# RWKV-7 recurrence and SwiGLU feed-forward on one core: copies of chunks 0 to 3 and a step of the weights' narrowing on GpSimd, token loads of chunks 1 to 3 on SyncE, another written-out order

## Chip, cores and metric

The kernel runs on one core of one Trainium2 chip. The metric is device time in microseconds of one execution of the whole program, as the median of several runs. Engines are named as the profile names them: PE (TensorE, PEld its weight loads), DVE (VectorE), ACT (ScalarE), POOL (GpSimd) and SP (SyncE, which here only issues DMAs).

## The reference

Two parts follow each other. The first is a recurrence over 768 tokens for 4 x 8 heads of 40 dimensions, with a 40 x 40 state per head:

```
for t in range(S):
    y[:, :, t] = einsum('bhd,bhde->bhe', r_t, state)
    Sa = einsum('bhde,bhe->bhd', state, a_t)
    state = state * w_t[:, :, None, :] - einsum('bhd,bhe->bhde', Sa, b_t) \
            + einsum('bhd,bhe->bhde', v_t, k_t)
```

The second takes y as 3072 rows of 320: x / sqrt(mean(x*x) + 1e-6) * rms_g, then silu(xn @ w_gate) * (xn @ w_val) @ w_out with 1536 hidden columns. The three weight matrices come as 64-bit floats, the other inputs as 32-bit.

## The kernel before, in words

The recurrence is cut into 24 chunks of C = 32 tokens, and for each chunk the work is written in stages:

- `front(c)` loads the chunk's tokens (tiles `wan`, with w and a; `kbn`, with k and b; `VU`, with v), turns them on PE, and builds what does not depend on the state. It runs through five levels, l = 1, 2, 4, 8, 16. At each level ACT copies keys from `K` into `KE`, PE makes a `gram` of `KE` and `A`, DVE writes its lower part into `LT` (a predicated copy, `where`), ACT copies another part into `KN`, DVE multiplies `K` in place, and the next level's `A` is made (at l = 16 it is `aP`). Half of the next `A` is the old one's values, moved to other places: the kept half, a copy of 128 x 256 elements on ACT (`copy(a1...)`, lines 513 and 523). The other half is a product on DVE. After the last level two copies of 128 x 512, `e0` and `e1` (lines 541 and 542), bring the last-level keys into `KE`; PE turns `KE`, and ACT copies the result into `KN` 32. There is one tile `KE`, so the next chunk's first key copy must wait for that turn.
- `inverse(c)` and, for chunks 0 to 3, `early_inverse(c)` invert the chunk's triangular matrices: `LT` goes out to the DRAM tile `sB` and comes back as `M`, DVE runs a chain of small products and subtractions (`tmp`, `M` or `Yi`), and the result goes out through `sY` and back.
- `main(c)` needs the state after chunk c - 1, the inverse and `front(c)`; it updates the state, makes `y`, the squared sum (`ss`), `x`, and the scaled and turned `xg`.
- `narrow(f, h)` makes 32-bit weights of half of weight tile `w` f, 24 halves in all: loads issued by POOL into a tile that is not yet in use, three steps of the exponents on ACT (into `ex`, or `o` where that tile is lent; lines 772 to 774), and three steps on DVE.
- `feed(g)` is the feed-forward part for two chunks, 12 in all: 12 weight tiles each, matmuls `ps<-xg,w`, silu on ACT (`sg`), product on DVE (`hT`), and `po<-w,hT`. The first, `feed(0)`, needs `main(0)` and `main(1)`.

None of it is issued as it is written. Every piece of work goes into a `Plan` with its engine, and `ORDER`, a table of numbers written out by hand or by a program, says in which order the pieces are issued; `PAIRS` says in which of three pairs of PSUM banks a temporary stands. Each engine works through its own pieces in that order and waits on semaphores for the others. A word "-" in `ORDER` issues a warming matmul on PE (`po<-ident`, line 1010), which computes nothing that is used.

Helpers, by whose lines the profile groups work: `copy` (476), `scale` (479), `act` (473) on ACT; `tt`, `where`, `ts`, `stt` (all 453) on DVE; `ptt` (482), `pcopy` (485), `blank` (488) on POOL; `dma` (492); `mm` (495) and `flip` (498) on PE. Buffer numbers are left out in the profile; in order rows `K_128` is the first of two `K` tiles.

Which queue loads a chunk's tokens is decided in two lines: chunk 0 by SP and ACT, chunk 1 by SP except its `VU`, and all later chunks by POOL.

Of the kernel before, what the change touches and what calls it, by code (L numbers as in the profile page):

```python
# [18 lines left out]
C = 32  # L19
# [4 lines left out]
EARLY, LATE = 4, 6  # L24
# [9 lines left out]
363 362 58 54 55 60 59 56 6 5 391 44 46 28 133 4 39 7 8 40 72 53 10 196 364 367 9 368 68 57 365 193 27 11 13 366 185  # L34
188 184 74 73 69 75 373 12 14 15 369 388 380 70 189 16 17 18 66 183 71 81 80 372 79 84 389 83 42 - - 82 187 93 91 88 76
90 182 78 89 92 20 41 195 34 262 35 85 94 186 321 65 77 102 98 99 103 64 100 87 399 201 43 203 86 101 104 108 109 263
202 477 473 398 95 97 110 476 472 114 105 198 470 475 107 113 112 96 115 197 390 474 118 106 116 199 129 126 117 119
130 111 212 125 222 232 200 120 124 123 - 242 121 211 131 204 134 210 132 208 209 205 - 220 206 213 214 219 207 489 381
471 218 217 223 63 127 128 221 215 824 823 228 227 51 229 233 224 231 67 225 230 819 820 226 491 490 240 237 241 29 320
238 194 30 371 234 216 236 243 239 135 62 61 136 137 138 139 140 141 142 248 143 486 - - 244 235 144 145 247 146 147  # L40
488 382 259 246 148 149 258 249 150 245 151 152 153 154 155 156 36 21 370 254 253 487 260 255 0 156 157 158 159 160 161
251 162 163 835 491 1006 821 1002 338 1007 18 391 392 492 836 496 165 166 37 164 167 249 498 495 837 500 260 497 499
493 121 494 506 310 - 504 505 508 168 501 256 394 509 510 519 507 515 502 311 255 384 321 511 382 373 263 514 518 376
817 512 517 516 520 503 377 264 265 525 521 513 176 172 174 170 177 816 323 374 44 178 169 173 171 175 179 523 375 250
47 31 30 266 267 268 269 524 270 21 530 46 957 526 191 820 528 529 385 522 180 378 383 399 531 534 545 393 312 - 36 313
324 407 32 405 315 537 271 272 532 956 386 395 314 316 325 535 416 533 - 317 408 415 322 326 329 549 49 318 546 330 331
336 400 402 527 273 274 275 276 396 277 278 279 538 280 281 282 283 284 540 541 285 286 287 288 289 290 333 335 403 547
401 339 417 404 332 337 334 342 344 838 2 539 1 291 423 406 548 409 340 190 189 341 420 292 345 421 542 543 544 484 550
551 832 294 426 412 552 553 834 293 410 554 346 347 413 481 425 424 434 411 414 427 536 844 418 295 - 343 348 349 833
# [5 lines left out]
468 580 879 958 615 614 621 887 886 582 0 263 92 - - 261 93 267 259 517 525 602 266 603 604 0 647 538 290 94 316 267 95  # L55
# [10 lines left out]
765 770 79 0 221 572 14 0 381 382 16 761 570 359 - 77 576 - 383 281 17 579 0 370 566 752 106 750 0 0 427 63 0 203 204  # L66
205 213 366 564 367 562 565 559 570 563 558 63 59 207 746 102 104 211 427 60 368 569 288 429 1 3 0 62 759 564 367 368 0
367 759 569 571 368 570 369 580 370 576 208 202 205 758 564 371 259 57 563 260 0 371 567 2 0 371 - 59 208 60 204 202
259 0 207 0 0 569 368 206 207 61 996 274 277 62 369 575 370 371 372 373 374 375 376 420 422 421 424 584 561 423 275 256
0 0 375 376 377 378 379 380 381 382 577 569 570 578 55 0 55 254 0 0 - 380 381 382 383 568 577 384 420 422 423 421 0 0  # L70
559 574 561 529 266 578 0 575 559 584 423 582 55 382 428 426 51 425 583 383 - 578 568 384 385 386 581 387 429 388 389
52 595 570 390 594 424 56 0 524 390 426 568 0 578 577 390 1 0 983 0 2 - 425 427 416 987 986 0 581 0 414 0 384 385 587
# [306 lines left out]
def kernel(  # L379
# [33 lines left out]
    nc = tc.nc  # L413
# [70 lines left out]
    def pcopy(o, a):  # L484
        plan.add("POOL", "copy", lambda at: nc.gpsimd.tensor_copy(o, a), [o], [a])
# [557 lines left out]
```

## Time and profile before

| | |
|---|---|
| median of 3 runs | 932.68 us (931.99 to 933.84) |
| the profiled execution | 934.37 us, of which 932.6 from the first to the last instruction |
| mean granted TensorE clock in it | 0.991 |
| busy in it: PE, PEld | 875.7 us (94%), 703.2 us (75%) |
| DVE, ACT, POOL | 723.2 us (78%), 521.9 us (56%), 294.9 us (32%) |
| DMA, mean over the span | 68 GB/s |

A profile shows one execution. Groups of instructions are given as: line, engine, operation, output tile <- input tiles, shapes, count, then busy time, mean duration of one in ns, and the engine's idle time just before, with what ended it. Rows of waits read: who waited, for whom, total us, times, longest. Rows of the timeline and the chain of waits begin with the start in us and the duration. Rows of stretches give each engine's busy time and, in brackets, its number of instructions. A busy PE is not PE at its peak, since ends of matmuls are modelled, and spans on POOL are rough.

### The profile page before, as it was taken

Reading aid. Unit: us, or ns where it says so; the run is one execution under the profiler, and the core shown is the slowest. Engines: PE = TensorE matmul, PEld = TensorE weight load, DVE = VectorE, ACT = ScalarE, POOL = GpSimd, SP = SyncE. Lnnn points to the kernel's source line nnn. Section 1 sums busy time; section 2 is a strip of 40 time slices with the busy share of each in tenths; the row PEclk is TensorE's granted clock in tenths of the full one; section 3 lists DMA queues with packets and bytes.
Section 4 is the critical chain, followed back from the end, with each engine's and each line's share of the span. In section 5 each row is a group of like instructions: output and inputs, shape, how many; then the busy total and the mean of one; then the engine's idle time right before and its main releaser. Section 6 shows DMA issues by size and latency. Waiting matters only on the chain.

```text
span 932.6 us, 50195 instructions
## 1 busy us (share of the span) xinstructions
PE 875.7 (94%) x22072; PEld 703.2 (75%) x22072; DVE 723.2 (78%) x2702; ACT 521.9 (56%) x1144; POOL 294.9 (32%) x515
## 2 busy tenths in 40 slices
PE   4776898899999999999999999999999999999998
PEld 4665776677777788777777887887787777878776
DVE  5887778878878888978888888888888887864511
ACT  5887877674555566565555655655545454432211
POOL 8576546404221323432221333412503320200000
PEclk9999999899999999999999999999999999999999
DMA  9653546223242243333323223413414222021000
GB/s 162 104 119 84 126 98 153 73 69 67 55 87 49 46 86 73 71 59 60 70 39 74 64 54 75 89 35 71 88 21 85 61 41 62 11 60 28 3 15 15
DMA packets 146363, 63.01 MB, mean 68 GB/s; under 512 B 128800, under 2 KB 138080, under 8 KB 146144
## 3 DMA queue, kind: packets, MB, share of 16 engines
q1 hardware_dynamic: 125664, 29.46, 17.1%
q0 software_dynamic: 18368, 30.01, 15.1%
q8 instruction: 173, 2.83, 1.3%
q10 hardware_dynamic: 2112, 0.33, 0.3%
q14 instruction: 46, 0.38, 0.1%
HBM read 49.15 MB, written 10.09 MB: 64 GB/s over the span
## 4 chain that ended last, share of the span: by engine, by line
PE 72%; DMA 9%; DVE 6%; ACT 6%; issue 3%; SPq 2%; POOL 1%; DVEq 0%; POOLq 0%; ACTq 0%
PE ps L495 50%; PE po L495 14%; PE ps L498 7%; SPq L492 2%; DMA M<-sB 2%; DMA w<-in_moe_w_out_dram 1%; DMA LT<-sY 1%; DMA w<-in_moe_w_gate_dram 1%; DVE tmp L453 1%; DVE y L453 1%; DMA sY<-Yi 1%; ACT VU L476 1%; ACT KE L476 1%; DVE Yi L453 1%; DMA sY<-M 1%
## 5 line engine op out<-in xcount | busy, mean ns | idle before, releaser
L495 PE MATMUL ps<-xg,w 128*128 128x256 f32 (+1 forms) x1728 | 354.2, 393 | 1.2 <-DVE Yi L453 0.5
L495 PEld LDWEIGHTS ps<-xg,w 128*128 128x128 f32 (+1 forms) x1728 | 263.7, 191 | 49.1 <-issue 12.4
L495 PE MATMUL po<-w,hT 128*128 128x320 f32 x576 | 179.0, 449 | 0.0
L492 POOL DMA_DIRECT2D VU<-in_v_dram x184 | 102.4, 560 | 172.7 <-PE ps L495 78.1
L453 DVE TENSOR_TENSOR tmp<-Yi,M 128x60 f32<-128x60 f32 (+24 forms) x620 | 129.3, 209 | 20.5 <-DMA M<-sB 6.1
L453 DVE TENSOR_TENSOR Yi<-Yi,tmp 128x60 f32<-128x60 f32 (+24 forms) x620 | 129.7, 210 | 13.8
L473 ACT ACTIVATE sg<-ps 128x256 f32<-128x256 f32 x144 | 52.6, 384 | 150.6 <-PE ps L495 143.1
L495 PEld LDWEIGHTS po<-w,hT 128*128 128x128 f32 x576 | 106.0, 192 | 37.4 <-issue 1.9
L476 ACT COPY KE<-K 128x512 f32<-128x512 f32 x168 | 110.6, 662 | 26.2 <-DVE K L453 18.2
L453 DVE TENSOR_TENSOR hT<-ps,sg 128x256 f32<-128x256 f32 x144 | 58.3, 420 | 68.7 <-ACT sg L473 57.4
L453 DVE TENSOR_TENSOR K<-K,T 128x256 f32<-128x256 f32 x240 | 98.9, 421 | 10.2 <-ACT KE L476 8.8
L495 PE MATMUL ps<-A,KE 40*64 40x72 f32 x3840 | 95.0, 247 | 9.0 <-ACT KE L476 1.7
L495 PEld LDWEIGHTS ps<-A,KE 40*64 40x64 f32 x3840 | 79.2, 149 | 28.9 <-issue 9.3
L476 ACT COPY KN<-ps 128x320 f32<-128x320 f32 x144 | 67.4, 471 | 59.1 <-PE ps L495 28.5
L453 DVE COPY_PREDICATED LT<-msk,ps 128x256 f32<-128x256 uint32 x120 | 65.9, 550 | 19.5 <-PE ps L495 10.2
L482 POOL TENSOR_TENSOR ss<-ss,mhalf 128x1 f32<-128x1 f32 x24 | 15.4, 641 | 194.2 <-DVE ss L453 179.2
L453 DVE TENSOR_TENSOR y<-y,ps 128x256 f32<-128x256 f32 x119 | 49.9, 419 | 11.0 <-PE ps L495 7.9
L453 DVE TENSOR_TENSOR A<-A,T 128x128 f32<-128x128 f32 (+1 forms) x168 | 55.8, 335 | 1.5 <-ACT A L476 0.4
L495 PEld LDWEIGHTS ps<-As,KN 64*40 64x40 f32 x3840 | 45.1, 123 | 12.7 <-issue 4.4
L495 PE MATMUL ps<-As,KN 64*40 64x32 f32 x3840 | 50.3, 204 | 3.1 <-DVE y L453 1.6
L476 ACT COPY VU<-ps 32x320 f32<-32x320 f32 x96 | 40.0, 417 | 15.5 <-PE ps L495 14.2
L492 POOL DMA_DIRECT2D wan<-in_w_dram x44 | 29.1, 661 | 57.4 <-PE ps L498 57.1
(121 smaller groups left out, 1250.2 us busy)
## 6 DMA issues: line engine op xcount, KB each, us to landing
M<-sB SPq DMA_DIRECT2D x80, 128.0 KB, 3.4
rn<-in_r_dram SPq DMA_DIRECT2D x24, 160.0 KB, 4.6
out_dram<-o SPq DMA_DIRECT2D x48, 80.0 KB, 2.3
VU<-in_v_dram POOLq DMA_DIRECT2D x184, 20.0 KB, 2.6
kbn<-in_b_dram POOLq DMA_DIRECT2D x44, 80.0 KB, 3.4
kbn<-in_k_dram POOLq DMA_DIRECT2D x44, 80.0 KB, 3.3
wan<-in_w_dram POOLq DMA_DIRECT2D x44, 80.0 KB, 3.1
wan<-in_a_dram POOLq DMA_DIRECT2D x44, 80.0 KB, 3.3
```

The lines of the kernel that those rows point to most:

```text
L453: plan.add("DVE", kind, lambda at: fn(at(o), *m(at)), [o], aps(*args))
L473: plan.add("ACT", "act", lambda at: nc.scalar.activation(at(o), at(a), f, **kw), [o] + aps(acc), [a])
L476: plan.add("ACT", "copy", lambda at: nc.scalar.copy(at(o), at(a)), [o], [a])
L482: plan.add("POOL", "tt", lambda at: nc.gpsimd.tensor_tensor(o, a, b, op), [o], [a, b])
L492: plan.add(by, "dma", lambda at: queue.dma_start(out=o, in_=i), [o], [i])
L495: return o, lhsT, rhs, lambda at: nc.tensor.matmul(at(o), lhsT, rhs, start=start, stop=stop, skip_group_check=True)
L498: return o, i, ident, lambda at: nc.tensor.transpose(at(o), i, ident)
```

## The change

A new constant, `SOON = 4`. For chunks 0 to 3, `front` makes the kept halves of `A` (and `aP`) and the two last-level key copies `e0` and `e1` with `pcopy`, on POOL, where it used `copy`, on ACT: 5 + 2 copies for each chunk, 28 in all. For chunks 1 to 3 all token loads are issued by SP: 8 more `VU` loads of chunk 1, and 8 token loads and 8 `VU` loads of each of chunks 2 and 3, 40 in all, leave POOL's queue. The last of the three exponent steps of `narrow`, a multiplication of integers by 2 to the 23rd, goes from ACT to POOL for all 24 halves. And `ORDER` and `PAIRS` are other tables.

```
-EARLY, LATE = 4, 6
+EARLY, LATE, SOON = 4, 6, 4
...
-0 225 226 223 0 0 0
+222 226 223 224 225 0 - 0 0
...
+    def pts(o, a, by, op):
+        plan.add("POOL", "ts", lambda at: nc.gpsimd.tensor_scalar(o, a, by, None, op), [o], [a])
...
     def tokens(t, i, x, src, tk, by="SP"):
-        dma(..., by if tk.start == 0 else "SP" if tk.start == C else "POOL")
+        dma(..., by if tk.start == 0 else "SP" if tk.start < SOON * C else "POOL")
...
     def front(c):
+        move = pcopy if c < SOON else copy
...
-                        "SP" if c == 0 else "POOL")
+                        "SP" if c < SOON else "POOL")
...
-                copy(a1[:, :, :, 0], a0[:, :, 0])
+                move(a1[:, :, :, 0], a0[:, :, 0])
...
-                copy(a1[:, :, :, :, 0], a0[:, :, 0].rearrange("p n f s l -> p n s f l"))
+                move(a1[:, :, :, :, 0], a0[:, :, 0].rearrange("p n f s l -> p n s f l"))
...
-        copy(e0, K[:, 0].rearrange("p (m n) (x t) -> p m n x t", m=2, x=2))
-        copy(e1, ap(K, N * 2 * C + C, (4 * 2 * C, 2), (2 * C, 4), (-C, 2), (1, C)))
+        move(e0, K[:, 0].rearrange("p (m n) (x t) -> p m n x t", m=2, x=2))
+        move(e1, ap(K, N * 2 * C + C, (4 * 2 * C, 2), (2 * C, 4), (-C, 2), (1, C)))
...
-        act(ex, ex, AF.Copy, scale=2.0 ** 23)
+        pts(ex, ex, 2.0 ** 23, MUL)
```

The tables move pieces on every engine. Three places show how. PE's pieces are the same in number and kind, 28 warming matmuls among them.

ACT, before, from the end of chunk 0's front (keys `K_128`, `KN_0`) into chunk 1's (`K_129`):

```order
L476 COPY KE<-K_128 128x2x4x2x32
L476 COPY KN_0_117<-ps_65 128x320
L476 COPY KE<-K_128 128x2x4x2x32
L476 COPY A_132<-ps_64 128x8x64
L476 COPY aP_133<-A_131 128x16x16
L476 COPY KE<-K_129 128x512
L476 COPY A_131<-A_132 128x8x32
```

ACT, in the changed kernel, from the same level of chunk 0 to the same first key copy of chunk 1:

```order
L477 COPY KN_0_117<-ps_65 128x320
L477 COPY KN_0_114<-ps_64 128x320
L474 ACTIVATE o_170<-w_164,ctop 128x480
L474 ACTIVATE ex_172<-w_163,ctop 128x480
L474 ACTIVATE o_170<-o_170,cmid 128x480
L477 COPY KE<-K_129 128x512
```

The two key copies, the `aP` copy and chunk 1's first `A` copy are no longer on ACT, and exponent steps of two weight tiles stand ahead of chunk 1's first key copy.

POOL, before, while chunk 0's front is made: loads of tokens of chunk 2 and of weights:

```order
L492 DMA kbn_96<-in_b_dram 32x16x40 x2
L492 DMA w_162<-in_moe_w_gate_dram 128x2x256
L492 DMA kbn_96<-in_k_dram 32x16x40 x2
L492 DMA wan_95<-in_w_dram 32x16x40
L492 DMA wan_95<-in_a_dram 32x16x40
L492 DMA VU_99<-in_v_dram 32x4x40
L492 DMA w_165<-in_moe_w_gate_dram 64x256
```

POOL, in the changed kernel, from the end of chunk 0's front into chunk 1's:

```order
L489 COPY KE<-K_128 128x2x4x2x32 x2
L489 COPY aP_133<-A_131 128x16x16
L496 DMA w_165<-in_moe_w_gate_dram 64x256
L496 DMA w_162<-in_moe_w_out_dram 128x448
L489 COPY mid<-msk 128x256
L489 COPY M_135<-ident 32x8x16
L496 DMA w_162<-in_moe_w_gate_dram 128x2x256
L489 COPY A_131<-A_132 128x8x32
L489 COPY A_132<-A_131 128x8x16x2
```

The token loads are gone from POOL; the copies stand there among loads of weights and the filling of constants.

SP, before, where chunk 0's `LT` goes out to `sB_173` and comes back as `M_135`:

```order
L492 DMA sB_173<-LT_102 32x8x32 x4
L492 DMA VU_98<-in_v_dram 32x4x40
L492 DMA M_135<-sB_173 32x16x16 x2
L492 DMA VU_98<-in_v_dram 32x4x40
L492 DMA rn_97<-in_r_dram 64x16x40
```

SP, in the changed kernel, there:

```order
L496 DMA sB_173<-LT_102 32x8x32 x4
L496 DMA kbn_96<-in_k_dram 32x16x40
L496 DMA VU_98<-in_v_dram 32x4x40
L496 DMA wan_95<-in_a_dram 32x16x40
L496 DMA wan_95<-in_w_dram 32x16x40
L496 DMA M_135<-sB_173 32x16x16
L496 DMA kbn_96<-in_k_dram 32x16x40
L496 DMA M_135<-sB_173 32x16x16
```

Token loads of chunks 2 and 3, which wait until PE has turned the chunk before and so freed their tile, now stand between the two transfers.

More of the change, by code (lines that the diff above doesn't have):

```diff
@@ new lines @@
+235 144 145 146 487 488 245 147 148 247 149 386 150 392 393 246 151 152 194 66 - 836 311 312 259 249 258 260 193 321
[5 rows of a table added]
+405 533 280 281 282 283 284 285 286 326 524 534 318 327 330 331 332 337 - 287 425 408 426 427 428 535 288 289 290 291
+292 293 431 319 818 2 190 822 328 429 340 335 333 334 338 191 821 48 1007 453 546 547 336 540 295 341 432 342 294 329
+548 343 344 296 409 410 411 1008 430 433 346 347 348 542 297 195 541 192 349 413 52 435 412 350 833 839 834 414 415 345
+549 835 452 847 843 23 857 481 543 - 1020 840 1021 454 842 351 352 353 957 1001 1006 844 848 841 867 354 538 599 434
@@ new lines @@
+298 444 463 484 482 537 846 544 442 460 355 845 302 443 854 356 1022 436 853 545 480 552 855 553 554 455 555 456 556
+600 849 856 852 864 49 858 866 306 862 601 863 457 877 437 851 865 557 - 859 1005 445 462 558 559 560 561 876 304 850
[4 rows of a table added]
+272 271 270 274 275 276 293 277 278 659 0 309 660 317 316 2 1 272 278 659 293 904 535 671 279 280 533 532 540 0 157 - -
[6 rows of a table added]
+76 12 366 - 265 364 184 77 254 579 369 267 377 565 313 372 371 370 376 269 268 263 78 271 270 0 14 15 579 12 265 580
+263 372 373 374 378 575 272 274 0 12 15 16 305 17 773 0 377 579 224 273 271 269 0 78 273 274 275 278 276 277 16 770 1
@@ new lines @@
+17 574 378 279 767 769 126 224 306 307 768 2 379 380 79 225 226 381 363 280 19 382 281 282 383 384 20 283 80 227 18 0
+307 227 581 570 0 263 427 - 558 63 562 561 99 564 0 363 364 558 564 565 559 206 210 211 102 574 569 571 59 60 566 - -
+568 570 575 427 567 573 365 366 367 743 744 1 429 368 369 263 63 264 66 370 265 64 584 572 371 580 372 3 0 0 0 0 260
+206 201 203 207 65 573 0 569 0 259 260 570 577 206 0 0 0 0 571 - 49 55 565 577 361 578 362 363 364 365 366 367 570 368
+369 583 203 60 569 257 204 205 260 258 53 749 0 0 749 368 369 370 748 257 577 416 371 372 373 374 580 375 376 377 991 1
@@ new lines @@
+741 783 784 988 785 989 0 434 617 828 832 439 830 829 785 786 787 788 831 835 995 789 440 836 833 834 790 - 991 791 792
+793 992 1008 993 839 1093 794 840 795 796 841 797 - 435 798 842 799 845 847 846 1138 1394 682 943 939 844 800 441 801
[7 rows of a table added]
+1195 0 545 592 593 655 594 651 746 654 595 652 747 596 4 657 656 658 653 597 598 660 743 659 760 599 744 600 - 0 600
[28 rows of a table added]
+1159 817 818 819 820 430 - 1217 1166 1 683 1083 1084 1086 1170 1171 1167 1174 1026 1027 1028 1029 1176 1172 863 864 434
+1030 1181 824 822 1031 1185 1032 1033 1195 1034 1180 441 1169 - 436 1186 823 437 1035 865 866 867 1168 1036 821 1087
@@ L242 @@
-42220044024200200400200442020422400000444420204
+20404240010220204445204204204422440242244040404244202242200042024014540040400402404000202000444220020022004420404204044
+42000044422042242400000224200402242242242224420444444204404240424020244240024040240002240000422444400402442204040242240
+44440444040240220240444444002400422402422202040024222442024200042024420400420024024242040440044222200002002424224422042
+20442200020042442420440204424444200020424224424402422440204240202240422400440400404244424202022404022000002200244400022
@@ L243 @@
+22000402002022002244004204444224424444240240042
 """
@@ L657, in tokens @@
     def tokens(t, i, x, src, tk, by="SP"):
-        dma(flat(t)[rows(i, x), :, 0:D], src[2 * i:2 * i + 2, :, tk, :].rearrange("q h s d -> s (q h) d"), by if tk.start == 0 else "SP" if tk.start == C else "POOL")
+        dma(flat(t)[rows(i, x), :, 0:D], src[2 * i:2 * i + 2, :, tk, :].rearrange("q h s d -> s (q h) d"), by if tk.start == 0 else "SP" if tk.start < SOON * C else "POOL")
     def front(c):
```

53 lines of the change are left out of this document (14 added, 39 removed), and 332 rows, old and new, of the table ORDER.

## The prediction

> **What bounds the kernel now.** I read the table of stretches first, cut at the first matmul (9.6 us), at the first matmul of the feed-forward part (112.4 us) and at 193 us, when the last weights are narrowed.
>
> ```profile
> 0.00:9.60 9.60, 0.00 (x0) 0.00 (x1) 2.68 (x7) 3.09 (x4) 8.30 (x27) 1.00 0.83 139
> 9.60:112.40 102.80, 77.14 (x2213) 66.96 (x2213) 83.60 (x277) 83.25 (x174) 64.80 (x119) 1.00 0.62 118
> 112.40:193.00 80.60, 73.18 (x1943) 57.59 (x1940) 65.34 (x218) 59.42 (x122) 41.25 (x69) 0.94 0.47 105
> 193.00:932.60 739.60, 725.41 (x17920) 578.69 (x17920) 571.60 (x2204) 376.16 (x847) 180.50 (x302) 1.00 0.28 55
> 112.39 3.79 PE L495 MATMUL ps<-xg,w 64*128 64x256 f32 x16
> ```
>
> After the length, the columns are busy time of PE, PEld, DVE, ACT and POOL, then the granted clock. PE does nothing for 9.6 us, idles 102.8 - 77.1 = 25.7 us in the second stretch, which I call the ramp, and then 7.4 and 14.2 us. PE's work is not touched by the change (as many matmuls, as many warming ones), so the end moves only by what PE's idle time gains or loses, and nearly half of that (25.7 of 56.9) is in the ramp. There DVE (83.6) and ACT (83.3 of 102.8) are both about 81% busy, and POOL 63%.
>
> Next the table of waits, for the ramp alone: first PE's, then DVE's.
>
> ```profile
> PE ps L498 <- DVE y L453: 4.1, 2, 2.5
> PE ps L495 <- ACT M L476: 3.6, 3, 2.7
> PE ps L498 <- ACT KE L476: 2.4, 2, 1.6
> PE ps L498 <- ACT VU L476: 2.4, 2, 1.7
> PE ps L495 <- ACT KE L476: 1.7, 2, 1.2
> PE ps L495 <- ACT A L476: 1.5, 2, 1.0
> PE ps L495 <- ACT KN L476: 1.5, 2, 1.0
> PE ps L498 <- ACT vut L476: 1.2, 1, 1.2
> PE ps L498 <- ACT r L476: 1.0, 1, 1.0
> ...
> DVE K L453 <- ACT KE L476: 4.4, 4, 3.2
> DVE w L453 <- ACT ex L473: 3.4, 1, 3.4
> DVE As L453 <- ACT As L479: 1.9, 1, 1.9
> DVE ss L453 <- ACT x L473: 1.1, 1, 1.1
> ```
>
> The eight ACT rows of PE add up to 15.3 of its 25.7 us; the DVE row is 4.1. DVE itself idles 102.8 - 83.6 = 19.2 us, and its four ACT rows are 10.8 of them. So in the ramp ACT is most often what is late. The chain of waits shows why, where chunk 0's front ends and chunk 1's begins:
>
> ```profile
> 24.28 0.62 ACT KE L476
> ...
> 25.22 0.52 ACT KE L476
> 25.74 0.49 ACT A L476
> 26.23 0.31 ACT aP L476
> 26.54 0.86 ACT KE L476
> ```
>
> From 24.28 on ACT does one copy after another, and PE's next gram waits for the last (26.54 and 0.86 long). Those of 0.62, 0.52 and 0.31 us, at 24.28, 25.22 and 26.23, are among the ones that the change moves.
>
> **The change, part by part.** ACT loses, for chunks 0 to 3, 20 kept-half copies (tiles A and aP), 8 key copies (KE), and one of three exponent steps of every half weight tile, 24 in all.
>
> ```profile
> L476 ACT COPY KE<-K 128x512 f32<-128x512 f32 x28 | 18.5, 660 | 6.1 <-PE ps L495 3.1 <-DVE K L453 2.9
> L476 ACT COPY A<-A 128x256 f32<-128x256 f32 x16 | 6.8, 422 | 0.3 <-DVE A L453 0.3
> L473 ACT ACTIVATE ex<-ex 128x480 int32<-128x480 int32 x8 | 4.8, 604 | 0.1
> ```
>
> All 28 copies and 12 of the exponent steps stand ahead of the first feed: 20 x 0.422 + 8 x 0.660 + 12 x 0.604 = 21 us. ACT's instructions overlap at their ends (the chain counts 0.31 for an aP copy), so I take 17 us off its busy time: 83.3 becomes 66, and its free time in the ramp 19.5 becomes 36.5. If waits behind ACT fell only as its load, PE would get back 15.3 x 17 / 83.3 = 3.1 us; if they went altogether, 15.3. A queue's waits go rather as busy time over free time, 4.3 before and 1.8 after, which leaves 0.43 of them: I take 15.3 x 0.57 = 8.8 us, and 3.1 and 15.3 as ends.
>
> The rows of ACT's order in the section on the change show the place of that chain: the two key copies, the aP copy and the first A copy of chunk 1 are gone from ACT, and steps for weights fill their place. The key copies are not off the path, though: both must be done before PE can turn KE, and only then may K_129's copy write KE again. On ACT the pair took 25.74 - 24.28 = 1.5 us, with a KN copy in the part left out.
>
> POOL takes them. What it does with such shapes, and what its DMA issues cost, the groups of POOL in the ramp show:
>
> ```profile
> L492 POOL DMA_DIRECT2D VU<-in_v_dram x14 | 8.0, 569 | 0.4 <-PE ps L495 0.4
> L567 POOL TENSOR_SCALAR_AFFINE_SELECT eye<-eye 32x256 f32<-32x256 f32 x4 | 2.0, 509 | 0.3
> L485 POOL COPY mid<-msk 128x256 f32<-128x256 f32 x3 | 1.3, 431 | 1.6 <-DVE msk L453 1.6
> ```
>
> A kept half is a copy of 256 elements: 0.43 us, as on ACT. A key copy has 512: between 0.51, the select's time for 256, and twice 0.43 (0.86); I take 0.65, since some of 0.43 is fixed, so the pair is 1.3 us against 1.5. No row has an integer multiply on POOL; 480 elements lie between 0.51 again and the select scaled up (0.509 x 480 / 256 = 0.95); I take 0.70, near what 0.65 for 512 and a slower operation make. Before the first feed the change has 28 copies and 14 exponent steps on POOL: 20 x 0.43 + 8 x 0.65 + 14 x 0.70 = 23.6 us (19.8 to 28.8 by the ends). 32 loads leave POOL there, by the VU row at 0.57 us or more: 18 us. POOL so goes from 64.8 to about 70 of 102.8 and does not become the bound; but its new work stands in line with loads that wait. In the rows of POOL's order, token loads, which waited for PE to free their tiles, are replaced by copies; but the load into w_162, which waits until DVE has narrowed what lay there, stands ahead of chunk 1's A copies. I charge 1 us for copies held up so, with 0 and 5 as ends.
>
> The larger cost is on DVE. Rows of the timeline, POOL's copies beside DVE's work:
>
> ```profile
> 13.14 0.40 POOL L485 COPY mid<-msk 128x256 f32<-128x256 f32 x1 [1.59 <-DVE msk L453]
> 13.49 0.65 POOL L485 COPY A<-ident 40x320 f32<-40x320 f32 x1
> 13.31 1.10 DVE L453 TENSOR_TENSOR K<-K,T 128x256 f32<-128x256 f32 x2 [0.30 <-ACT T L476]
> 19.06 0.76 DVE L453 TENSOR_TENSOR K<-K,T 128x256 f32<-128x256 f32 x2 [0.16 <-ACT KE L476]
> 33.19 0.54 POOL L488 MEMSET y<- 128x512 f32 x1
> 33.18 0.49 DVE L453 TENSOR_TENSOR A<-A,T 128x128 f32<-128x128 f32 x2
> ```
>
> Under two POOL copies (1.05 us) the pair of K products took 1.10 us instead of 0.76: 0.34 lost, 0.32 us for each us of copying. Under a memset, which reads nothing, the A products ran on at 0.49 for two. At 0.32 the new reading on POOL costs DVE 23.6 x 0.32 = 7.6 us in the ramp; the ends are 0 (copies that fall into DVE's idle time) and 14.4 (below). What PE sees of it is less, since PE waits less for DVE than for ACT: I take half, 3.8 us.
>
> The 40 loads on SP:
>
> ```profile
> 11.18 0.98 SPq L492 DMA_DIRECT2D kbn<-in_k_dram  x2
> ...
> sB<-LT SPq DMA_DIRECT2D x16, 32.0 KB, 3.4
> ```
>
> 0.49 us each, 20 us on a queue that mostly waits. In the rows of SP's order four loads now stand between sB_173 and the first M_135; 4 x 0.49 = 2.0 us is covered by the 3.4 us that the sB transfer needs to land. I charge nothing; without that cover, as when a load there waits for PE to free its tile, it is 2 us, twice, for the two inverses ahead of the first feed: 4 us.
>
> After 112.4 us ten or twelve exponent steps leave ACT too, with 7.4 us of PE's idle time to be had in that stretch; I charge nothing there, with -2 to +2 as ends, since DVE (65.3 of 80.6) is the busier.
>
> **The sum**, made against the profiled execution: its span of 932.6 us and 1.8 around it make 934.37, 0.2% over the median of the runs, 932.68. The terms are -8.8 (ACT) + 3.8 (DVE) + 1 (POOL's line) + 0 (SP) = -4.0 us; 930.4 against the profiled execution, 928.7 against the median, which I forecast.
>
> **The rivals.** First, slower: **POOL's reads hold up DVE.** If every copy blocks DVE for as long as it runs whenever DVE wants two operands, DVE loses 23.6 us times its busy share (0.81) times the share of such work. That share is bounded by the groups of DVE in the ramp that do not read two tiles of SBUF (LT's reads its mask and PSUM):
>
> ```profile
> L453 DVE COPY_PREDICATED LT<-msk,ps 128x256 f32<-128x256 uint32 x20 | 10.9, 547 | 5.2 <-PE ps L495 4.6 <-ACT KN L476 0.4
> L453 DVE TENSOR_SCALAR w<-w 128x480 int32<-128x480 int32 x13 | 5.8, 449 | 3.4 <-ACT ex L473 3.4
> L453 DVE TENSOR_TENSOR y<-y,ps 128x256 f32<-128x256 f32 x9 | 3.8, 419 | 2.2 <-PE ps L495 2.1
> ```
>
> These are 20.5 of 83.6, so the share is at most 0.755 and the loss 23.6 x 0.81 x 0.755 = 14.4 us. DVE gets back 10.8 x 0.57 = 6.2 of its waits for ACT; if DVE sets the ramp, the end comes 8.2 us later: 940.9. It decides from 6.2 / 23.6 = 0.26 us of DVE for each us of POOL upward, if DVE and not ACT is then what is late; the measured 0.32 is just over that, DVE's share of PE's waits speaks against. The Trainium skill, "SBUF — State Buffer", section "Who interferes with whom", says that a DVE instruction with two SBUF inputs and a GpSimd instruction that reads SBUF exclude each other entirely, while one that only writes does not matter. By that rule this rival is what happens; the trace agrees on both halves (1.10 instead of 0.76 us beside copies, 0.49 for two beside a memset). Chance 0.25.
>
> Second, **no difference**: the same balance at 0.32 gives DVE +7.6 - 6.2 = +1.4 us, and with DVE 81% busy before, a freer ACT only moves the wait: 932.7 to 934.1. Chance 0.17, counting as no difference what is within 0.2% (1.9 us), about what a measurement of this kernel can tell.
>
> Third, **faster by more**: PE gets nearly all its ACT waits back (-15.3), POOL's copies fall into DVE's free time, and 3 us are charged for all else: -12, 920.7. For it speaks that the line of copies on ACT at each change of chunk is cut short; against it, that PE can turn KE only after the same key copies. Chance 0.13.
>
> Fourth, **lines on POOL and SP**: A copies behind loads that wait for DVE (5), M behind token loads (4), against half the ACT gain (-4.4): +4.6, 937.3. Chance 0.08.
>
> **How the numbers follow.** The forecast, 924 to 931, has 0.37. Faster by over 0.2%: 0.37 + 0.13 = 0.50; within: 0.17; slower: 0.25 + 0.08 = 0.33. Both signs hold much of this, so the range takes in the third rival's value and the first's: 920 to 941, with about 0.15 outside.
>
> **What would show it.** Right: in the changed profile the first xg matmul starts about 4 us before 112.4, PE's waits ended by ACT in the ramp fall from 15.3 to about 6.5, KE copies of 512 elements take about 0.65 us on POOL and exponent steps about 0.7, K products beside them are lengthened by about a third of POOL's time. Wrong: the first feed at 112 us or later with DVE over 92 us busy before it and PE's waits now ended by DVE or POOL (first rival); rows of A or aP on POOL that start long after their input is there, with a load ahead (fourth); exponent steps well over 1 us, which would make POOL the bound; or a gain of the ramp that comes back as PE idle time between 112 and 193 us.

## The result: 27 us slower, and where the profile shows it

The changed kernel takes 959.76 us (median of 4 runs, 957.10 to 965.79) against 932.34: a ratio of 1.0301, 95% interval 1.0263 to 1.0340. I had forecast 928.7, and 920 to 941 as the range. The profiled execution took 960.75 us, of which 958.8 are its span.

The table of stretches of the changed kernel, cut at the first matmul of the feed-forward part (121.8) and at the end of `feed(0)`'s last output matmul (230.2); columns as in the prediction (length, busy PE, PEld, DVE, ACT, POOL, granted clock):

```profile
9.60:121.80 112.20, 75.81 (x2191) 65.35 (x2187) 95.44 (x278) 69.40 (x137) 84.36 (x131) 1.00 0.60 110
121.80:230.20 108.40, 93.77 (x2398) 73.41 (x2396) 79.74 (x258) 63.87 (x137) 55.19 (x72) 0.87 0.38 87
230.20:958.80 728.60, 714.27 (x17473) 569.35 (x17472) 559.29 (x2153) 366.05 (x818) 177.95 (x298) 1.00 0.27 54
```

The same view of the kernel before, from its first feed to the same matmul:

```profile
112.40:206.10 93.70, 85.66 (x2299) 67.40 (x2296) 76.11 (x254) 69.63 (x148) 43.57 (x73) 0.95 0.45 102
```

The first feed comes 9.4 us later, not 4 earlier: PE idles 112.2 - 75.8 = 36.4 us there instead of 25.7, less 1.3 us of work that it now does ahead of 9.6. Between the cuts it idles 14.6 instead of 8.0 us, +6.6. Over the whole span its idle time goes from 56.9 to 73.6 us, +16.7, and its busy time, for the same matmuls, from 875.7 to 885.2, +9.5. 16.7 + 9.5 are the 26.2 us of the two spans. The second part I put down to the clock, 0.87 between the cuts instead of 0.95: 0.13 x 108.4 less 0.05 x 93.7 is 9.4 us that half clock took more, an estimate from these rows, which takes it that all of PE's work there is paced by the clock.

POOL's groups up to 125 us have the new work:

```profile
L486 POOL TENSOR_SCALAR ex<-ex 128x480 int32<-128x480 int32 x9 | 13.3, 1479 | 3.5 <-ACT ex L474 3.4
...
L489 POOL COPY A<-A 128x256 f32<-128x256 f32 x16 | 9.2, 574 | 8.5 <-DVE A L454 5.6 <-DVE T L454 0.9 <-PE ps L499 0.8
...
L486 POOL TENSOR_SCALAR o<-o 128x480 int32<-128x480 int32 x5 | 7.2, 1442 | 5.1 <-ACT o L474 5.0
L489 POOL COPY KE<-K 128x512 f32<-128x512 f32 x8 | 5.6, 707 | 5.6 <-PE ps L499 3.3 <-DVE K L454 1.5 <-DVE tmp L454 0.8
```

The exponent step takes 1.44 to 1.48 us, twice the 0.70 that I took and well over my upper end of 0.95; on ACT it was 0.60. The 14 of them are 20.5 us of POOL.

And the waits from 9.6 to 121.8 us, the first rows of PE's and of ACT's:

```profile
PE ps L499 <- ACT KE L477: 6.3, 4, 2.6
PE ps L499 <- ACT M L477: 4.1, 4, 2.0
PE ps L499 <- ACT rE L477: 4.0, 1, 4.0
...
ACT KE L477 <- DVE K L454: 12.4, 10, 2.1
ACT K L477 <- PE ps L502: 8.0, 3, 6.2
```

PE's waits ended by ACT did not shrink, though ACT's load fell as forecast: three rows alone are 14.4 us, against 15.3 for the eight rows of ACT before, and PE now waits for copies on POOL too (4.2 us). ACT itself waits for DVE's K products ahead of its key copies (12.4 us; 2.9 before), so the row names the last engine of a chain, not the slow one.

### The profile page after: what moved, and what is told of

Same layout as the page of the kernel before. It is cut to its first block, busy times and chain, and to the rows that moved or that the text cites. A ratio compares the mean times of both kernels' runs of the same rounds, so it can differ in the third digit from the quotient of the medians.

```text
span 958.8 us, 50223 instructions
## 1 busy us (share of the span) xinstructions
PE 885.2 (92%) x22072; PEld 709.3 (74%) x22072; DVE 739.6 (77%) x2702; ACT 501.6 (52%) x1092; POOL 326.3 (34%) x527
## 4 chain that ended last, share of the span: by engine, by line
PE 68%; DVE 10%; ACT 8%; DMA 7%; issue 3%; POOL 2%; SPq 1%; ACTq 0%; DVEq 0%; POOLq 0%
PE ps L499 47%; PE po L499 14%; PE ps L502 7%; DMA kbn<-in_k_dram 2%; ACT VU L477 2%; DVE tmp L454 2%; SPq L496 1%; DVE w L454 1%; DVE K L454 1%; ACT KE L477 1%; DVE LT L454 1%; DVE hT L454 1%; DVE Yi L454 1%; ACT KN L477 1%; DMA sY<-M 1%
## 5 line engine op out<-in xcount | busy, mean ns | idle before, releaser
L496 POOL DMA_DIRECT2D VU<-in_v_dram x160 | 88.7, 558 | 143.7 <-PE ps L499 88.1
L477 ACT COPY KE<-K 128x512 f32<-128x512 f32 x160 | 105.8, 662 | 50.5 <-DVE K L454 40.9
L454 DVE TENSOR_TENSOR K<-K,T 128x256 f32<-128x256 f32 x240 | 99.5, 424 | 15.3 <-ACT KE L477 9.6
L477 ACT COPY KN<-ps 128x320 f32<-128x320 f32 x144 | 67.2, 469 | 73.6 <-DVE LT L454 29.0
L499 PE MATMUL ps<-As,KN 64*40 64x32 f32 x3840 | 53.2, 206 | 9.5 <-DVE y L454 3.8
L454 DVE TENSOR_TENSOR y<-y,T 128x256 f32<-128x256 f32 x96 | 41.5, 433 | 2.8 <-ACT y L477 1.2
```

Of the source, the lines that this page charges most:

```text
L454: plan.add("DVE", kind, lambda at: fn(at(o), *m(at)), [o], aps(*args))
L477: plan.add("ACT", "copy", lambda at: nc.scalar.copy(at(o), at(a)), [o], [a])
L496: plan.add(by, "dma", lambda at: queue.dma_start(out=o, in_=i), [o], [i])
L499: return o, lhsT, rhs, lambda at: nc.tensor.matmul(at(o), lhsT, rhs, start=start, stop=stop, skip_group_check=True)
```

## The experiments

Times are given as a ratio to the kernel before on the same chip, with its 95% interval, and as that share of 932.7 us.

### Which part costs what

Four kernels: the new tables (`ORDER`, `PAIRS`) with parts of the moves undone, and the old tables with one part. Exponents back on ACT, in the changed kernel:

```
-        pts(ex, ex, 2.0 ** 23, MUL)
+        act(ex, ex, AF.Copy, scale=2.0 ** 23)
```

> The changed kernel with one line undone: the exponents' last step is on ACT again; copies on GpSimd, loads on SyncE and the new order stay. Theory E (the exponent step, 1.4 to 1.5 us on POOL where I had 0.70, is the cause: it fills POOL and holds DVE): at least half of the 27 us comes back, 933 to 946 us, first feed at 112 to 116 us, DVE lengthened by 7 us instead of 15. Theory P (each read of POOL blocks DVE, the copies as much as the exponents): about half of it, 944 to 952. Theory O (the new order and the loads on SP lose it): within 4 us of the changed kernel, 956 to 964, since ACT only gets its 14 us of work back.

Measured: 953.86 us, 1.0209 (1.0186 to 1.0232), 19.5 us. It lies between what P and what O gave (952 and 956), and none of the three is met: about 9 of the 28 us are the exponents'.

Copies back on ACT, in the changed kernel:

```
-        move = pcopy if c < SOON else copy
+        move = copy
```

> The changed kernel with the kept halves and the key copies of chunks 0 to 3 on ACT again; the exponent step stays on GpSimd. Theory E: little comes back, 952 to 960, since POOL only goes from 81 to about 67 us busy before the first feed. Theory P: 940 to 950, DVE lengthened by 10 us instead of 15. Theory O: 956 to 966.

Measured: 964.82 us, 1.0322 (1.0294 to 1.0351), 30 us; not told apart from the changed kernel, in O's range.

New tables alone: both edits above, and

```
-        dma(..., by if tk.start == 0 else "SP" if tk.start < SOON * C else "POOL")
+        dma(..., by if tk.start == 0 else "SP" if tk.start == C else "POOL")
...
-                        "SP" if c < SOON else "POOL")
+                        "SP" if c == 0 else "POOL")
```

> The new order alone: exponents and copies on ACT, token loads of chunks 2 and 3 on GpSimd as before. Theory O: it keeps at least half of the loss, 946 to 965. Theories E and P: the order costs little by itself, 930 to 940; above 934 because the order was made for other engines.

Measured: 961.66 us, 1.0295 (1.0272 to 1.0318), 27.5 us, in O's range. The tables lose by themselves all that the change loses.

The kernel before, with only the exponents' step on POOL:

```
-        act(ex, ex, AF.Copy, scale=2.0 ** 23)
+        pts(ex, ex, 2.0 ** 23, MUL)
```

> The kernel before, in its own order, with only the exponents' last step on GpSimd. Theory E: slower by half of the 27 us or more, 946 to 965, with POOL at 64.8 + 14 x (1.4 to 1.6) = 84 to 87 us busy before the first feed. Theory P: 940 to 948 (35 us of reading at 0.22 to 0.32 us of DVE each, half of it in the ramp). Theory O: 928 to 936, no loss without the new order.

Measured: 966.41 us, 1.0347 (1.0312 to 1.0381), 32 us, just above E's range. So the exponents too lose by themselves all that the change loses, in the old order. The two do not add. The other parts in the old order, each with the lines of the change's diff for it; first all moves, without the new tables:

```
+        dma(..., by if tk.start == 0 else "SP" if tk.start < SOON * C else "POOL")
...
+        move = pcopy if c < SOON else copy
...
+                        "SP" if c < SOON else "POOL")
...
+                move(a1[:, :, :, 0], a0[:, :, 0])
...
+                move(a1[:, :, :, :, 0], a0[:, :, 0].rearrange("p n f s l -> p n s f l"))
...
+        move(e0, K[:, 0].rearrange("p (m n) (x t) -> p m n x t", m=2, x=2))
+        move(e1, ap(K, N * 2 * C + C, (4 * 2 * C, 2), (2 * C, 4), (-C, 2), (1, C)))
...
+        pts(ex, ex, 2.0 ** 23, MUL)
```

> The kernel before, in its own order, with all three moves (copies and exponents on GpSimd, 40 loads on SyncE): the whole change but for its tables. Theory Q (the exponent steps make a line on POOL: they wait there for ACT, and loads of weights and all else of POOL behind them): 960 to 975, as with the exponents alone (966.4). Theory O (the new tables lose it by themselves, whatever the engines): faster than the changed kernel by over 10 us, under 950; but the exponents alone already speak against that. A third, T (the new tables were made for the moves, and make them cheaper than the old order does): over 960, since 959.8 is what the same moves cost in the order made for them.

Measured: 965.64 us, 1.0361 (1.0311 to 1.0411), 34 us, as Q and T had it; O's number fails.

Of that diff only the five lines with `move`:

> The kernel before, in its own order, with only the kept halves and key copies of chunks 0 to 3 on GpSimd. By my prediction's terms without the exponents: ACT loses about 11 of its 14 us of copies, so 15.3 x 11 / 83 to 15.3 x 0.4, a gain of 2 to 6 us, less 3 for DVE and 1 for the line: 927 to 934. Theory Q: POOL's line in the old order (loads that wait stand ahead of copies on PE's path) costs more than that: 936 to 950. Theory P (each copy blocks DVE): 934 to 940.

Measured: 938.55 us, 1.0045 (1.0013 to 1.0076), 4 us slower: above what my terms gave, in the ranges of P and Q.

Only the two lines with `SP`:

> The kernel before, in its own order, with only the 40 loads of chunks 1 to 3 on SyncE. My prediction took 0, with 4 as the end: 931 to 937. Theory Q: POOL's line gets shorter by 32 loads ahead of the first feed, a gain of 0 to 4: 929 to 933. Against: SP's own line, loads that wait for PE ahead of M's transfers, 936 to 945.

Measured: 934.09 us, 0.9997 (0.9969 to 1.0026): nothing, as forecast.

The lines with `move` and those with `SP`:

> The kernel before, in its own order, with the copies on GpSimd and the loads on SyncE, exponents on ACT: the change without its exponents and without its tables. Theory Q: the copies gain when no token loads stand ahead of them on POOL: 924 to 932, faster than either alone. Theory P: 934 to 940, since DVE is held as before.

Measured: 935.73 us, 1.0023 (0.9995 to 1.0050): 2 us, at the edge of what can be told from none: P's range, and not faster than either alone by what can be measured.

| moved | old tables | new tables |
|---|---|---|
| nothing | 1 | 1.0295 |
| copies, loads | 1.0023 | 1.0209 |
| exponents, loads | | 1.0322 |
| exponents | 1.0347 | |
| all | 1.0361 | 1.0301 |

Read down, copies and loads gain 8 us in the new tables (1.0295 to 1.0209, intervals apart) and nothing in the old. Exponents cost 32 us in the old tables (1.0023 to 1.0361 gives as much) and 8.6 in the new (1.0209 to 1.0301), where POOL waits less for ACT ahead of them: 27.7 us from 9.6 to 240 us, against 58.3 with all moves in the old tables. The parts don't add in the new tables either: with the exponents on POOL the copies bring 2 us (1.0322 to 1.0301, not told apart), and without the copies exponents and loads cost 2.5 (1.0295 to 1.0322, not told apart). All moves together cost 0.6 us there.

### Where the new tables lose

Engines and queues as before; the old table up to the first feed's matmul, then the rest of the pieces as the new table has them:

```
-ORDER = new
+ORDER = old[:746] + [pieces of new that are left, in its order]
```

> Engines and queues as in the kernel before; the old order up to the first matmul of the feed-forward part, the new order for all that is left. Theory R (the new order loses its 28 us in the ramp, where it holds back chunk 1's inverse): 930 to 937. Theory L (the ramp costs 13 us, the other 15 are lost by the new order after it): 943 to 952.

Measured: 953.92 us, 1.0215 (1.0177 to 1.0252), 20 us. The reverse:

```
-ORDER = new
+ORDER = new[:759] + [pieces of old that are left, in its order]
```

> The reverse: engines and queues as before, the new order up to the first matmul of the feed-forward part, then the old order. Theory R: 955 to 965, all of the loss. Theory L: 943 to 949, the 13 us of the ramp alone.

Measured: 947.35 us, 1.0150 (1.0119 to 1.0181), 14 us, as L said (the first of the two is 2 us above L's range). The first feed starts at 125.2 us in this run and at 112.0 in the other. The new tables lose about 14 us ahead of the first feed, and 14 to 20 after it; R falls. (Both runs have `PAIRS` of their own, and 25 and 31 warming matmuls instead of 28; what that costs was not taken apart.)

Then an attempt to mend the first half. In the changed kernel chunk 1's inverse ends later; the timeline of PE shows its two groups of matmuls and what follows them, before:

```profile
82.00 0.68 PE L495 MATMUL ps<-M,LT 32*16 32x16 f32 x58 [0.52 <-DMA M<-sY]
85.41 1.12 PE L495 MATMUL ps<-M 16*32 16x16 f32 x64 [2.73 <-ACT M L476]
86.90 0.36 PE L495 MATMUL ps<-Xs,M 32*32 32x40 f32 x8 [0.36 <-ACT M L476]
```

and after the change:

```profile
94.12 0.72 PE L499 MATMUL ps<-M,LT 32*16 32x16 f32 x64 [0.72 <-DVE tmp L454]
...
98.09 0.35 PE L499 MATMUL ps<-Xs,M 32*32 32x40 f32 x8 [1.24 <-ACT M L477]
```

It is 11 us late at the product with Xs. Its transfers are mixed with token loads, and PE has three grams of chunk 3 ahead of it. The first repair puts all that it needs after DVE's part close together; of POOL's rows the memset of M moves:

```
 DMA w_165<-in_moe_w_val_dram 64x256
-COPY M_136<-ident 32x8x16
+MEMSET M_136 128x8x32
+COPY M_136<-ident 32x8x16 x2
 DMA kbn_96<-in_k_dram 32x16x40
...
 DMA w_162<-in_moe_w_gate_dram 128x2x256
-MEMSET M_136 128x8x32
 DMA w_163<-in_moe_w_gate_dram 64x256
```

> The changed kernel, with one thing moved in its order: what chunk 1's inverse needs after DVE's part (one scaling on ACT, 11 transfers on SP, one memset and one filling of constants on POOL, two groups of matmuls on PE and two copies) stands close together again, ahead of token loads, chunk 2's transfers and two grams of chunk 3; engines and queues as in the change. Theory R: chunk 1's inverse ends at 88 to 91 us instead of 98, the first feed starts at 113 to 116, and the time is 950 to 954. If the inverse is not what holds the ramp: 957 to 963.

Measured: 970.17 us, 1.0402 (1.0352 to 1.0452): 10 us slower than the changed kernel, and outside both ranges. Its timeline of POOL has the reason:

```profile
66.96 0.52 POOL L498 DMA_DIRECT2D w<-in_moe_w_val_dram  x1
74.49 0.32 POOL L494 MEMSET M<- 128x256 f32 x1 [7.00 <-DMA sY<-M]
```

I had put the memset where POOL comes 7 us before its transfer has landed, and all of POOL's line (key copies, kept halves, loads) stood behind it. To see whether the copies in that line were the harm, the same repair with engines and queues as before:

> The new order alone (engines and queues as before) with the same repair of chunk 1's inverse as in the changed kernel. Theory Q (there POOL's wait of 7 us for the inverse's transfer held the key copies and kept halves behind it; on ACT they are free of it): the repair now helps, 950 to 957 against 961.7. If the repaired order is simply worse: 965 to 973.

Measured: 967.71 us, 1.0381 (1.0344 to 1.0418), slower than without the repair (1.0295), and not what Q said. So it wasn't the copies alone; token loads and weights stood in that line too. The second repair leaves the memset later; PE's rows:

```
 MATMUL ps_63<-VU_99,LT_103 32x40 x32
-MATMUL ps_65<-A_131,KE 64x72 x16
-MATMUL po<-ident 128x128
-MATMUL ps_64<-A_132,KE 64x72 x16
-MATMUL ps_63<-A_131,KE 64x72 x16
 MATMUL ps_65<-M_136,LT_103 16x16 x32
-MATMUL ps_65<-M_136 32x16 x32
+MATMUL ps_65<-A_131,KE 64x72 x16
+MATMUL ps_64<-M_136 32x16 x32
+MATMUL po<-ident 128x128
+MATMUL ps_64<-A_132,KE 64x72 x16
+MATMUL ps_63<-A_131,KE 64x72 x16
 MATMUL ps_65<-Xs_143,M_136 32x40 x32
```

> The changed kernel with chunk 1's inverse repaired once more: transfers out close together where they were; the memset, the filling and the 8 transfers back stand later on POOL and SP than in the first repair, behind chunk 2's key copies and chunk 3's token loads, so that POOL should wait no more than 1 or 2 us there; matmuls and copies as in the first repair. Theory R (the inverse's scattered line holds the ramp): it ends at 88 to 91 us instead of 98, first feed at 113 to 117, 949 to 955. If something else is as late: 956 to 963.

Measured: 965.13 us, 1.0361 (1.0319 to 1.0403), no better than the changed kernel, and above both ranges. PE's timeline in it:

```profile
90.05 0.36 PE L501 MATMUL ps<-M,LT 32*16 32x16 f32 x25 [2.91 <-issue]
...
92.04 1.05 PE L501 MATMUL ps<-M 16*32 16x16 f32 x64
...
96.55 1.24 PE L501 MATMUL ps<-A,KE 40*64 40x72 f32 x32 [0.52 <-issue]
98.42 1.29 PE L501 MATMUL ps<-Xs,M 32*32 32x40 f32 x64 [0.63 <-DVE tmp L456]
101.77 1.42 PE L501 MATMUL ps<-A,KE 40*64 40x72 f32 x32 [2.06 <-ACT KE L479]
```

The inverse's matmuls run about 4 us earlier, but the product with Xs starts at 98.4 as before: the grams of chunk 3, which used to stand ahead of the inverse, now stand between it and its user (which then waits another 0.63 us for DVE), and the next gram, too, waits on PE's only line for its keys while `main(1)` stands behind it. Moving one chain forward in a line moves the other back. So what exactly makes the new tables 14 us longer in the ramp isn't settled; that it isn't chunk 1's inverse alone is.

### What the exponent step costs on POOL

In the kernel before, a memset in the step's place: same row in POOL's line as the multiplication had, same wait for ACT, but 0.50 us and nothing read. The multiplication is left out.

```
-        act(ex, ex, AF.Copy, scale=2.0 ** 23)
+        blank(ex, 1 << 23)
```

> The kernel before, in its own order, with a memset on GpSimd in the place of the exponents' last step: it stands in POOL's line and waits as the multiplication did, but takes about 0.5 us instead of 1.55 and reads nothing. It leaves the multiplication out. Theory Q (what costs 32 us is the line: the step waits there for ACT, loads behind it): 953 to 966. Theory D (the duration, 14 x 1 us more of POOL ahead of the first feed, and DVE held by the reading): 934 to 945.

Measured: 952.98 us, 1.0212 (1.0179 to 1.0246), 20 us: the lower end of Q, and far from D. Three memsets in a row, together as long as the step (the lines of the helper that issues them):

```
+            for _ in range(3):
+                nc.gpsimd.memset(o, value)
```

> The kernel before in its own order, with three memsets on GpSimd in the place of the exponents' last step: about 1.5 us, as long as the multiplication, but nothing read. It leaves the multiplication out. If the step's length in POOL's line is what its price adds to its place: 962 to 968, as with the multiplication. If it is the reading, which holds DVE: 951 to 957, as with one memset. Between them the two share it.

Measured: 963.87 us, 1.0346 (1.0303 to 1.0389), 32 us, as good as the multiplication's 1.0347. So of its 32 us the place in the line is 20 (with whatever ACT gains by being rid of the step already taken off), its length 12, and the reading nothing that shows; the two intervals leave some 5 us either way. The stretch up to the first feed, with the multiplication and with the memsets:

```profile
9.60:123.20 113.60, 76.77 (x2212) 66.57 (x2210) 85.90 (x277) 77.44 (x162) 85.88 (x133) 1.00 0.55 107
```

```profile
9.60:123.70 114.10, 77.18 (x2214) 67.13 (x2214) 85.00 (x277) 77.61 (x163) 84.24 (x157) 1.00 0.56 107
```

DVE's 277 instructions take 85.9 and 85.0 us. What the place does, the waits of the exponents' run (the multiplication in the old order) from 9.6 to 240 us show, POOL's, ACT's and PE's:

```profile
POOL ex L485 <- ACT ex L473: 32.9, 13, 6.8
POOL o L485 <- ACT o L473: 18.2, 5, 6.8
```

```profile
ACT o L473 <- DMA w<-in_moe_w_val_dram: 10.8, 2, 7.0
...
ACT o L473 <- POOL y L491: 6.0, 1, 6.0
...
ACT ex L473 <- DMA w<-in_moe_w_gate_dram: 4.3, 1, 4.3
```

```profile
PE ps L498 <- ACT KN L476: 9.3, 4, 7.0
PE ps L498 <- ACT M L476: 8.3, 5, 6.2
```

POOL stands 51 us waiting for ACT's second step; behind it stand the loads of the next weights; ACT, in its own order, then waits up to 7.0 us for such a load, and PE up to 7.0 us for a KN copy that stands behind that on ACT. A ring of lines. In the kernel before, with the step on ACT, ACT waits no longer than 1.9 us for such a load in this stretch, and PE no longer than 1.0 us for KN. One turn of the ring in the timelines of POOL, ACT and PE:

```profile
141.43 1.47 POOL L485 TENSOR_SCALAR o<-o 128x480 int32<-128x480 int32 x1 [6.84 <-ACT o L473]
...
149.87 0.72 POOL L495 DMA_DIRECT2D w<-in_moe_w_val_dram  x1
```

```profile
153.12 0.72 ACT L473 ACTIVATE o<-w,ctop 128x480 f32<-128x480 int16 x1 [7.04 <-DMA w<-in_moe_w_val_dram]
```

```profile
154.20 2.08 PE L498 MATMUL ps<-xg,w 64*128 64x256 f32 x8 [6.96 <-ACT KN L476]
```

If it is so, a later place must help; each step issued a few pieces ahead of the DVE product that uses it, which moves 15 of the 24 steps (the edit of the table, in short):

```
+    L.remove(step); L.insert(L.index(user) - 12, step)   # where that is later
```

> The kernel before in its own order, exponents' last step on GpSimd as in the run that took 966.4, but each of these steps issued later, a few pieces ahead of the product of DVE that needs it, so that loads pass it in POOL's line. Theory Q (the wait for ACT in POOL's line): 942 to 953, most of the 20 us of the memset run comes back. Theory D (duration and reading): 960 to 968.

Measured: 957.08 us, 1.0263 (1.0230 to 1.0296): 8 us come back, less than Q said and more than D, so the ring is shown in part. POOL still waits 44 us for ACT there.

### PE's clock

Rows of 4 us of the changed kernel (length, busy PE first, clock behind POOL's):

```profile
152.00:156.00 4.00, 1.92 (x93) 1.57 (x80) 2.01 (x6) 2.16 (x6) 3.00 (x5) 1.00 0.87 194
156.00:160.00 4.00, 2.08 (x32) 2.01 (x33) 2.39 (x6) 1.44 (x3) 0.00 (x0) 0.61 0.81 226
160.00:164.00 4.00, 4.00 (x50) 2.67 (x53) 0.66 (x1) 1.55 (x4) 2.69 (x3) 0.54 0.04 8
164.00:168.00 4.00, 3.08 (x165) 2.33 (x163) 1.83 (x5) 3.24 (x6) 4.00 (x8) 1.00 0.77 204
...
172.00:176.00 4.00, 1.67 (x66) 1.29 (x66) 2.03 (x4) 0.59 (x1) 4.00 (x4) 0.74 0.23 31
176.00:180.00 4.00, 3.76 (x38) 3.17 (x39) 3.81 (x11) 1.44 (x3) 2.75 (x5) 0.50 0.44 73
```

There are four places from 150 to 220 us where PE is busy for about half of a few us and its clock is then at half. By the trace's clock records it is at half for 6.83 us each time, after 3.41 us in which PE was busy for 0.48, 1.29, 1.87 and 2.07 us. Before the change there is one such place, of 10.24 us. What it does to a matmul of `feed` stands in the row by tile (ns least, median, most):

```profile
L499 PE MATMUL ps<-xg,w x1728: 376/379/793, 121.8 to 949.0; 128*128 128x256 f32 x121, 64*128 64x256 f32 x71
```

At half clock one takes 793 ns (at 177.4 us) where the median is 379. The Trainium skill, "TensorE: Matmul & The Clock Gate", section "What's actually happening", has the clock fall to half after an idle window of about 3.4 us and come back after a busy one. The trace agrees on the return (PE is busy for all of the last 3.41 us before each) and on the first place, where PE waits 3.99 us at a stretch; at the other three its longest single wait is 2.12 us, so there the clock falls with less idle time than that. I tried to fill the gaps:

```
 MATMUL ps_65<-xg_152,w_160 128x256 x4
+MATMUL po<-ident 128x128 x3
 MATMUL ps_64<-ST_101,aP_134 32x40 x32
```

(the second of six such places)

> The changed kernel with 15 more warming matmuls ahead of the six pieces for which PE waited between 153 and 213 us (4, 3, 2, 2, 2, 2); nothing else. Theory C (each gap of PE there halves its granted clock for 5 to 7 us, which is 9 of the 27 us): the clock stays at 1.00 from 150 to 220 us and the time is 950 to 955. If what PE waits for there sets the time, and not its clock: 957 to 963.

Measured: 992.88 us, 1.0649 (1.0593 to 1.0704): 33 us slower than the changed kernel, outside both ranges, and the clock still falls four times. The kernel before, with four (one of three places):

```
 MATMUL ps_63<-VU_99,KN_0_120 40x40 x32
+MATMUL po<-ident 128x128 x2
```

> The kernel before with 4 more warming matmuls between 167 and 180 us, ahead of the gaps after which its clock was at half from 177 to 188 us; nothing else. Theory C: the clock stays at 1.00 there and 2 to 5 us come back, 928 to 931. If the clock there costs nothing: 932 to 936.

Measured: 939.33 us, 1.0085 (1.0054 to 1.0116), 8 us slower, again outside both ranges. The first run's loss isn't where the matmuls were added: `feed(0)` ends at 231.6 us (230.2 without them). Most of it comes from 370 us on, in waits of PE that nothing in the profile explains; of 370 to 945 us, with the added matmuls:

```profile
PE ps L501 <- issue: 16.2, 11, 2.3
PE ps L504 <- issue: 6.5, 6, 2.2
PE po L501 <- issue: 1.7, 2, 1.1
```

and in the changed kernel:

```profile
PE ps L499 <- issue: 2.5, 2, 2.2
```

So whether filling the gaps would bring the 9.5 us of clock back was not measured. No version that was run is faster than the kernel before by what can be measured.

## Why the prediction was wrong, step by step

- **The sum had no term for the tables: this is the step that failed.** I priced the moves at the three places that I had read in the order, as if the rest of the table only carried them. The tables alone are +27.5 us; in them copies and loads then bring 8 us and the exponents cost 8.6, which makes the measured 28. Both orders put the same work ahead of the first feed (DVE 277 and 278 instructions), so its load, which I summed, says nothing of it; the difference lies in what stands ahead of what. Which pieces of the tables do it stays open.
- **ACT, -8.8.** The load was about right (69.4 us busy, forecast 66). The rule from load to waits failed: PE's waits for ACT did not fall to 6.5, since ACT now waits for DVE. The gain itself is real in the new tables, where copies and loads bring 8 us, and none in the old.
- **The exponent step, 0.70 us.** It is 1.44 to 1.48. I had no row of an integer multiply and took a select of floats, scaled up, as the upper end; that is no bound for another operation. The copies were a little short too (0.57 and 0.71 us where I took 0.43 and 0.65). POOL's load became 84.4 us, not 70; in the ramp it still has 28 us free, so it became the bound only through its line.
- **POOL's line, +1 (0 to 5).** This is the term of the moves that was mis-sized: the place alone is 20 us in the old tables, the length 12 more. I had looked at copies behind loads, not at loads behind a step that waits for ACT, with ACT waiting for those loads.
- **DVE, 7.6 us longer, half of it seen.** The changed kernel's 278 DVE instructions of the ramp take 95.4 us; with nothing moved they take, in the run of the tables alone (length, PE, PEld, DVE and so on),

```profile
9.60:125.20 115.60, 74.67 (x2185) 63.60 (x2183) 86.14 (x278) 86.52 (x178) 67.50 (x123) 0.98 0.55 107
```

  86.1. 9.3 us more, for 20.5 us of steps and 9.2 + 5.6 us in the two large groups of copies, is 0.26 for each us, near the 0.32. (With only the copies on POOL the new tables have 90.8 us, with only the exponents 90.9.) But it doesn't look as if it set the end: the first feed comes later still (125.5) without it.
- **SP, 0.** Right in the old tables: 0.9997. In the new ones the loads were not moved alone.
- **After 112 us, 0 (-2 to +2).** The largest miss beside the tables: +6.6 us of idle time, and 9.5 of clock, for which I had no term though the row of 112.4 to 193 us had 0.94.
- **The rivals.** The first (reading holds up DVE, 940.9) has the sign, and DVE's load that I named for it, but not the cause of what the exponents cost in the old tables: three memsets that read nothing cost as much as the multiplication. The rule that it stood on, of the Trainium skill, "SBUF — State Buffer", section "Who interferes with whom", has a DVE instruction with two inputs in SBUF and a GpSimd instruction that reads SBUF exclude each other; the trace shows DVE lengthened (by 9.3 us in the changed kernel, by 0.9 against the memsets in the old tables), but by a part of the reading time, and it decides nothing here. The fourth (lines on POOL and SP, 937.3, chance 0.08) is nearest in mechanism, and was sized at about a quarter of what the line costs in the old tables. That exponent steps "well over 1 us" would show it wrong was the sign that came.

Open are the tables' 28 us in detail, and how much of the second half the clock is. Differences under 5 us between two programs are also not to be explained one by one here, since PE's unexplained waits, described below, come to between 0 and 7.2 us in all programs but one.

## What to carry to other kernels

Price a step that moves to an idle engine by its place in that engine's line first: what it waits for there, what stands behind it, and whether that in turn feeds what it waits for. Here the place was 20 us and the step's length 12, with the engine still idle for a quarter of the time. A written-out order is a part of the change with a price of its own: time it alone, with everything else undone, before reading anything into the rest. And a bound from another operation's row is no bound.

## What the runs showed of the hardware that I had not expected

- **PE's unexplained waits stand at one place of every 256 instructions.** In the run with 15 more warming matmuls, 25 waits of over 0.3 us end without anything to wait for. Counted over all of PE's records in the trace (matmuls, weight loads, semaphore instructions), 24 of them, 30.3 us in all, stand 193 or 194 past a multiple of 256; the 25th (1.1 us) does not. The changed kernel has 2 such (2.6 us), the kernel before 1 (1.2), the others 0 to 5. Why that run has so many is open. One of them (2.91 us) fell into the inverse of the second repair.
- **The granted clock of the ramp's rows is no measurement.** The same pieces up to the first feed, in the tables alone and in the run that goes on with the old table:

```profile
40.00:125.20 85.20, 55.98 (x1810) 48.27 (x1812) 66.64 (x219) 63.69 (x132) 48.03 (x86) 0.98 0.46 98
```

```profile
40.00:125.20 85.20, 56.48 (x1821) 48.77 (x1818) 66.26 (x216) 64.05 (x133) 48.11 (x86) 0.55 0.48 100
```

  The clock is 0.98 in one and 0.55 in the other, yet PE's busy time is 56 us in both, and the first feed starts at 125.5 and 125.2. That doesn't mean that the clock is without effect there: the traces' records of it begin only at 118.1 us and at 45.0 us, and what lies ahead of the first record is counted as 1.00. How long the matmuls take tells more. Three times the 32 matmuls of a gram in the changed kernel, in the ramp, just before its clock falls to half at 197.82 us, and just after:

```profile
92.16 1.24 PE L499 MATMUL ps<-A,KE 40*64 40x72 f32 x32 [1.10 <-issue]
...
196.07 0.73 PE L499 MATMUL ps<-A,KE 40*64 40x72 f32 x32
...
198.47 1.24 PE L499 MATMUL ps<-A,KE 40*64 40x72 f32 x32 [1.25 <-DVE Yi L454]
```

  So the small matmuls of the recurrence are paced by the clock too, and in the ramp they run as at half. The kernel before has the same 1.24 us in its ramp, and its first record at 116.6 us: the 1.00 that its row of the ramp shows is not its clock either, and the clock is no difference between the two kernels there.
- **GpSimd's integer multiply** takes 1.40 us at least for 128 x 480, and 1.44 to 1.57 on average in the runs here, three times a memset of as many (0.50), while its copies took 0.57 for 256 and 0.71 for 512 elements beside other work.
